# Mamba2 scan and PReLU MLP: chunk pairs 4 and 5 in two token blocks on half of the partitions, B and C of pair 4 turned by VectorE

## Chip, cores and metric

The kernel runs on one core of a Trainium2 chip. The metric is the device time of one execution in microseconds (us). TensorE is called PE here, its weight load PEld, VectorE DVE, ScalarE ACT, GpSimd POOL and the queue that issues most transfers SP. The granted TensorE clock was 1.000 over the whole profiled execution.

## The reference

Two blocks follow one another: a Mamba2 state-space scan in chunks, and an MLP with a PReLU whose slope is given for each hidden feature. Shapes: x is 4 x 8 x 768 x 32 (batch, heads H, tokens S, head width D), a is 4 x 8 x 768, B and C are 4 x 8 x 768 x 16 (state width N), w_in is 256 x 2048, w_out 2048 x 256, alpha 2048.

```python
log_a = np.log(np.clip(a, 1e-06, 1.0))
for c in range(nc):
    cum = np.cumsum(la, axis=-1)
    L = np.exp(cum[:, :, :, None] - cum[:, :, None, :]) * causal
    CB = np.einsum('bhin,bhjn->bhij', Cc, Bc)
    y_intra = np.einsum('bhij,bhjd->bhid', CB * L, xc)
    y_inter = np.einsum('bhin,bhnd->bhid', Cc, state) * np.exp(cum)[:, :, :, None]
    y[:, :, sl] = y_intra + y_inter
    Bx = np.einsum('bhjn,bhjd->bhjnd', Bc, xc) * np.exp(cum[:, :, -1:] - cum)[:, :, :, None, None]
    state = np.exp(np.sum(la, axis=-1))[:, :, None, None] * state + np.sum(Bx, axis=2)
...
h = y_as_tokens @ w_in            # 3072 x 2048
g = np.maximum(h, 0.0) + alpha * np.minimum(h, 0.0)
out = g @ w_out                   # 3072 x 256
```

## The kernel before

**Chunks, pairs, groups.** The kernel uses chunks of Q = 128 tokens, 24 of them: 6 for each of 4 batches. Two neighbouring chunks are a pair (0 to 11; pairs 0 to 2 are batch 0, 3 to 5 batch 1 and so on), and two pairs are a group of 512 tokens (0 to 5). The scan of a pair yields its 256 rows of the MLP's input, in the tile xT. Pairs 0 and 1 have a code of their own. All order is written out by hand: each engine executes its instructions in the order in which the program emits them, and waits at each for what it needs.

**What a pair needs.** For each head, the decays L are made by a scan on VectorE (L561 or L567, "dec<-abc"): the row of a, broadcast to all partitions by a transfer (abc, from the DRAM scratch z), is multiplied up from a one that stands on the diagonal of an identity matrix in PSUM (ident_p, one half of the bank m5_bank). B and C are needed with the state dimension on the partitions (bc). PE multiplies them for the gram products CB (L731 or L742); VectorE multiplies these by the decays (L753); and PE multiplies the result by x (L787 or L805) and adds the products of C with the old state (L779 or L797) into the same banks, the y products. ScalarE copies them into xT (L815 or L817). The state sums (L618 or L629) take bn, which is B times the decay to the chunk's end (GpSimd, L533, `pair_loads`); VectorE adds the old state (L642), GpSimd masks the sum (L645). GpSimd also makes cd, which is C times the decay from the chunk's start (L682).

**Two forms.** Pairs 2 to 5 use the whole form: a chunk's 128 tokens lie on 128 partitions. Pairs 6 to 11 (`gp >= HALF`, HALF = NP // 2 = 6) use the half form: chunk k lies on the partitions of half k, its tokens in two blocks of 64 (j = 0, 1). Decays and gram products of token block 1 with the queries of block 0 are zero and are left out, so that a head has 192 columns (SQ) for a chunk and not 256 for two: scans are 128x192 instead of 128x256, products 128x384 instead of 128x512. The matmuls use 64 or 32 rows by 32 or 64 columns of the PE array at places given by `tile_position`, several of them side by side. In the half form, the states and cd of a chunk are needed on the other half of the partitions as well; `moved` (L685) copies them there, cd by ScalarE and the masked state by GpSimd. The diagonal in ident_p is rearranged for the half form by `halve_identity` (two ScalarE copies), once, after pair 5's last scan. The rows of the scratch z of batches 2 and 3 are SQ = 192 wide: 128 values, and 64 more that begin the second block anew.

**B and C turned.** Pairs up to 4 transpose them on PE (four 128x128, L669) and copy the bank out by ScalarE (L672). Later pairs (`turned = gp > GC`, GC = 4) load them a second time in another layout and turn 32x32 blocks on VectorE (`turn_bc`, L574); `turn_bc(gp + 1)` is issued at the end of pair gp's products, with the first two scans of pair gp + 1 behind it.

**Two phases.** In the first, to about 78 us, the weights are loaded and converted, and for group 0 the MLP runs f by f (hidden L1095, output L1142), with pairs 1 to 3 between. What is issued after step f = 14 is `pair_loads(4)` and the rows of batches 2 and 3. Then follow `token_sums(1)` (L1183, "xs") and the first stages of pair 4. In the second phase the groups 1 to 5 run as 4 quads each (`quad`, z = 0 to 3), a Strassen-like product scheme with 7 products: matmuls L1241 into the PSUM tiles A and Y (both "hp", the pool ps_h with 2 buffers) and at times Z ("ss", the pool ps_s with 2 buffers), PReLU (`prelu`: L1224 on ScalarE, then L1226 on VectorE), differences on GpSimd (L1288, L1298) and matmuls L1216 into banks. The callback `after(j)` places the stages of the pairs of the next group among a quad's steps, by the table `steps`: pair 4 in quads z = 0 and 1 of group 1, pair 5 in z = 2 and 3. The gram products take two ss tiles and two hp tiles (`spare`), so they wait until PReLU has read A and Y. In group 1, GpSimd has in addition sums of weights (`weight_sums`, L1171, by the table `late_sums`), four in the first quad and four in the third (one of the first on VectorE).

**Loads.** `load_pair` issues a pair's transfers on SP: pair 4 at f = 10, pair 5 at the start of the first quad, pair 6 in the second, pair 7 in the fourth.

Of the kernel before, what the change touches and what calls it, by code (L numbers as in the profile page):

```python
# [9 lines left out]
F32 = mybir.dt.float32  # L10
# [12 lines left out]
def kernel(  # L23
# [25 lines left out]
    nc = tc.nc  # L49
# [4 lines left out]
    batch, H, S, D = x.shape  # L54
# [11 lines left out]
    GC = 4  # L66
# [10 lines left out]
    WQ = 256  # L77
    HQ = Q // 2
    SQ = Q + HQ
    HALF = NP // 2  # L80
    assert H * N == P and HD == d_model and KC == 2 and R == CPB == 6
    assert NCH % GC == 0 and GT == 512 and NF % 8 == 0 and d_model <= WQ

# [65 lines left out]
    def load_spread(gp, b, c):  # L149

        for w, t in enumerate(loads["p", gp][1] if gp >= HALF else ()):
            rows = scratch["z", b // 2].rearrange("(b h c) t -> b c h t", b=2, h=H)
            for k in range(2):
                nc.sync.dma_start(
                    out=t[HQ * k : HQ * (k + 1), : 4 * SQ].rearrange("p (h t) -> p h t", h=4),
                    in_=rows[b % 2, c + k, 4 * w : 4 * w + 4].unsqueeze(0)
                    .to_broadcast([HQ, 4, SQ]))
        for k, t in enumerate(loads["p", gp][1] if gp < HALF else ()):
            rows = scratch["z", b // 2].rearrange("(b h c) t -> b c h t", b=2, h=H)[b % 2, c + k]
            nc.sync.dma_start(out=t.rearrange("p (h t) -> p h t", h=H),  # L160
                              in_=rows.unsqueeze(0).to_broadcast([P, H, Q]))
            yield

    def load_products(gp, ap):
# [5 lines left out]
    def load_pair(gp, decays=True, parted=False):  # L170


        b, c = divmod(2 * gp, CPB)
        turned = gp > GC
        nat = ldx.tile([P, 3, 2, H * N], F32, name="nat")
        xt = ldx.tile([P, 2, HD], F32, name="xt")

        ap = ldx.tile([P, 2 * Q], F32, name="ap")
        if gp == 0:
            load_a(ap, b, c)  # L180
        elif gp > NB:
            load_products(gp, ap)
        if gp == 0:
            load_rows(0, nc.scalar)
        abc = []
        if gp >= HALF:
            load_tokens(nat[:, 0], B[b], c * Q)
        def load_bc(k):
            ts = slice((c + k) * Q, (c + k + 1) * Q)
            for i, src in enumerate((B,) if turned else (B, C)):  # L190
                eng = nc.scalar if gp == 0 and i else nc.sync
                eng.dma_start(out=nat[:, i, k].rearrange("p (h n) -> p h n", h=H),  # L192
                              in_=src[b, :, ts, :].rearrange("h p n -> p h n"))

        def load_x(k):
            ts = slice((c + k) * Q, (c + k + 1) * Q)
            nc.sync.dma_start(out=xt[:, k].rearrange("p (h d) -> p h d", h=H),  # L197
                              in_=x[b, :, ts, :].rearrange("h p d -> p h d"))

        for k in range((1 if parted else 2) if gp < HALF else 0):  # L200
            load_bc(k)
            if gp >= NB:
                load_x(k)
        for k in range(2 if gp < NB else 0):
            load_x(k)
        if gp == 0:
            nc.scalar.dma_start(out=al_n, in_=moe_alpha.rearrange("(k p) -> k p", p=P))
            loads["a", 1] = prep.tile([P, 2 * Q], F32, name="a1")
            load_a(loads["a", 1], b, c + 2)
        for i, src in enumerate((B, C) if turned else ()):  # L210


            for e in range(2):
                first = src[b, e : e + 1, c * Q : (c + 2) * Q, :]
                nc.sync.dma_start(out=nat[:, 1 + e, i],
                                  in_=bass.AP(tensor=first.tensor, offset=first.offset,
                                              ap=[[2 * S * N, P // 32], [8 * N, 32], [1, 8 * N]]))
        for k in range(2 if gp >= NB else 0):
            abc.append(lda.tile([P, H * Q], F32, name="abc"))
        loads["p", gp] = nat, abc, xt, ap  # L220
        if gp >= HALF:
            load_tokens(xt, x[b], c * Q)
        if decays:
            for part in load_spread(gp, b, c):
                pass
        return lambda: load_bc(1), lambda: load_x(1)
# [194 lines left out]
    def halve_identity():  # L421

        for s in range(2):
            nc.scalar.copy(
                out=ident_p[0][HQ:].rearrange("p (a s t) -> p s a t", a=2, s=2)[:, s],
                in_=ident[HQ:, HQ * (1 - s) : HQ * (2 - s)].unsqueeze(1).to_broadcast([HQ, 2, HQ]))
# [45 lines left out]
    def rows_out(i):  # L472


        if i == 0:
            scratch["z", 0] = dr.tile([RW, Q], F32, name="z0")
            nc.sync.dma_start(out=scratch["z", 0], in_=held.pop("z"))
            return
        d0 = held.pop(i)[:, :SQ]
        rpf = prep.tile([RW, Q], F32, name="rpf")  # L480
        nc.vector.tensor_tensor_scan(out=rpf, data0=d0[:, :Q], data1=zeros[:RW], initial=1.0,
                                     op0=ALU.mult, op1=ALU.add)
        nc.vector.memset(d0[:, :1], 0.0)
        for key, t in (("z", d0), ("pf", rpf)):
            scratch[key, i] = dr.tile([RW, t.shape[1]], F32, name=f"{key}{i}")
            nc.sync.dma_start(out=scratch[key, i], in_=t)

    def rows_short(r):

# [31 lines left out]
    def pair_loads(gp):  # L521

        b, c = divmod(2 * gp, CPB)
        nat, abc, xt, ap = loads["p", gp]

        bn = work.tile([P, 2, H * N], F32, name="bn")
        i, bi = divmod(b, 2)
        if gp >= HALF:
            pj = prt[i].rearrange("p (j b m h) -> p j b m h", j=2, b=2, h=H)[:, :, bi, c // 2]
        else:  # L530
            pj = (prt[i if gp >= NB else "short"]
                  .rearrange("p (b h c) -> p b c h", b=2, h=H)[:, bi, c : c + 2])
        nc.gpsimd.tensor_tensor(  # L533
            out=bn.rearrange("p k (h n) -> p k h n", h=H),
            in0=nat[:, 0].rearrange("p k (h n) -> p k h n", h=H),
            in1=pj.unsqueeze(3).to_broadcast([P, 2, H, N]), op=ALU.mult)
        return bn
# [43 lines left out]
    def pair(gp):  # L581
# [27 lines left out]
        def added_halves(banks):  # L609


            dps = [t[:, : 4 * D].rearrange("p (k m) -> p k m", k=2) for t in banks]
            for j in range(2):
                for r in range(4):
                    rs, hs = slice(32 * r, 32 * r + 32), slice(2 * r * D, 2 * (r + 1) * D)
                    for k in range(nk):
                        ks = slice(HQ * k, HQ * (k + 1))
                        nc.tensor.matmul(dps[k][rs, k], bn[ks, j, rs], xt[ks, j, hs],  # L618
                                         start=False, stop=j == 1,
                                         tile_position=(HQ * k, 32 * r),  # L620
                                         skip_group_check=True)
            return dps
# [131 lines left out]
            if i == 1:  # L754
                yield
        if fine and gp + 1 < NP:
            if gp + 1 == HALF:
                halve_identity()
                halved.append(True)
            turn_bc(gp + 1)  # L760
        yield

# [660 lines left out]
    def convert_next(first=True, **kw):  # L1423


        i = done[0]
        if i < len(pieces):
            convert(*pieces[i], **kw)
            if first and i and i + 2 < len(pieces):
                convert_a(*pieces[i + 2])  # L1430
            if loaded[0] == i + 6:
                load_next()
        done[0] += 1
# [20 lines left out]
    for f in range(FIRST, NF):  # L1454
        if f in (5, 10):
            load_pair(3 + f // 10)
        if f == 5:
            load_rows(1)
        hidden(0, f)
        for part in range(2):  # L1460
            if part:
                if f <= 10:
                    ssm(2)
                if f >= 9:
                    ssm(3)
            for i in CONVERTED.get((f, part), ()):
                if isinstance(i, str):
                    convert_a(*pieces[int(i)])
                else:
                    convert_next(first=False)  # L1470
        if f == 14:
            bns[4] = pair_loads(4)
            rows_clamp(1)
            held["pr"] = rows_scan(1)
            rows_out(1)
        if f == 8:
            bns[3] = pair_loads(3)
        output(f - FIRST)
        if f in in_steps:
            weight_sums(wi, in_sums, 0, in_steps[f])  # L1480
    early[0] = None
    beside[GC] = m5_bank[0][:, : 2 * Q]
    token_sums(1)
    ssm(2 * GC // 2, 4)

# [94 lines left out]
```

## Time and profile before

| What | Value |
|---|---|
| time, median of 3 runs | 355.99 us (355.93 to 356.35) |
| the profiled execution, first to last instruction | 355.9 us |
| PE busy | 349.3 us (98%) |
| PEld busy | 284.4 us (80%) |
| DVE busy | 235.8 us (66%) |
| POOL busy | 204.4 us (57%) |
| ACT busy | 171.8 us (48%) |
| one half-form scan (L561, 128x192) | 522 ns, mean of 48 |
| one whole-form scan (L567, 128x256) | 664 ns, mean of 32 |
| one turn on DVE (L574, 128x512) | 1114 ns, mean of 7 |
| one product of the half form (L753, 128x384) | 548 to 553 ns |
| one product of the whole form (L753, 128x512) | 681 to 685 ns |

Of the span's other executions the profile tells nothing; the profiled one differs by 0.1 us from the median of the runs. Groups of instructions are named by line, engine, operation and tile, out<-in. A matmul in f32 is recorded as two passes, so counts of matmuls in the chain are twice those in the code. A busy PE is not PE at its peak: ends of matmuls are modelled.

### The profile page before, as it was taken

Reading aid. Unit: us, or ns where it says so; the run is one execution under the profiler, and the core shown is the slowest. Engines: PE = TensorE matmul, PEld = TensorE weight load, DVE = VectorE, ACT = ScalarE, POOL = GpSimd, SP = SyncE. Lnnn points to the kernel's source line nnn. Section 1 sums busy time; section 2 is a strip of 40 time slices with the busy share of each in tenths; the row PEclk is TensorE's granted clock in tenths of the full one; section 3 lists DMA queues with packets and bytes.
Section 4 is the critical chain, followed back from the end, with each engine's and each line's share of the span. In section 5 each row is a group of like instructions: output and inputs, shape, how many; then the busy total and the mean of one; then the engine's idle time right before and its main releaser. Section 6 shows DMA issues by size and latency. Waiting matters only on the chain.

```text
span 355.9 us, 7778 instructions
## 1 busy us (share of the span) xinstructions
PE 349.3 (98%) x2985; PEld 284.4 (80%) x2985; DVE 235.8 (66%) x482; ACT 171.8 (48%) x391; POOL 204.4 (57%) x228
## 2 busy tenths in 40 slices
PE   8899999999999999999999999999999999999996
PEld 4576665578788888888888888888888888888885
DVE  6876986998748756847747856757856633643363
ACT  3477576535355346345345445345445344443431
POOL 6776568589939855725646626637526535434520
PEclk9999999999999999999999999999999999999999
DMA  7899989607345403503423423422001001001102
GB/s 138 182 202 270 329 174 279 148 17 159 106 83 128 102 3 75 104 2 77 78 57 74 86 51 71 85 55 65 11 2 31 0 2 29 2 1 31 31 0 59
DMA packets 105581, 30.24 MB, mean 85 GB/s; under 512 B 79896, under 2 KB 101448, under 8 KB 105544
## 3 DMA queue, kind: packets, MB, share of 16 engines
q1 hardware_dynamic: 103048, 29.43, 36.3%
q10 hardware_dynamic: 2496, 0.32, 0.6%
q8 instruction: 23, 0.38, 0.5%
q14 instruction: 14, 0.11, 0.1%
HBM read 26.32 MB, written 3.42 MB: 84 GB/s over the span
## 4 chain that ended last, share of the span: by engine, by line
PE 89%; SPq 4%; DMA 3%; DVE 2%; ACT 1%; POOL 1%; issue 0%; DVEq 0%; ACTq 0%
PE bank L1216 33%; PE hp L1241 29%; PE bank L1142 6%; PE ss L1241 6%; PE hp L1095 3%; DMA raw<-in_moe_w_in_dram 2%; SPq L192 2%; PE ss L787 1%; PE ss L731 1%; PE hp L1110 1%; PE bank L1209 1%; PE ss L805 1%; PE ss L779 1%; DMA xt<-in_x_dram 1%; SPq L197 1%; PE ss L742 1%
## 5 line engine op out<-in xcount | busy, mean ns | idle before, releaser
L1298 POOL TENSOR_TENSOR gt<-gt 128x512 f32<-128x512 f32 x58 | 74.2, 1279 | 21.1 <-DVE gt L1226 16.3
L1216 PE MATMUL bank<-gt,w_out 128*128 128x256 f32 x320 | 83.5, 381 | 0.0
L1216 PEld LDWEIGHTS bank<-gt,w_out 128*128 128x128 f32 x320 | 60.1, 190 | 9.2 <-issue 1.0
L1288 POOL TENSOR_TENSOR gt<-gt 128x512 f32<-128x512 f32 x20 | 25.4, 1269 | 62.5 <-DVE gt L1226 49.7
L1226 DVE SCALAR_TENSOR_TENSOR gt<-hp,s_mul,gt 128x256 f32<-128x256 f32 x96 | 42.0, 479 | 29.1 <-ACT gt L1224 26.8
L1224 ACT ACTIVATE gt<-hp,s_alpha 128x256 f32<-128x256 f32 x96 | 40.3, 471 | 34.5 <-PE hp L1241 31.4
L1216 PE MATMUL bank<-gt,ws 128*128 128x256 f32 x224 | 55.9, 379 | 0.0
L1216 PEld LDWEIGHTS bank<-gt,ws 128*128 128x128 f32 x224 | 42.3, 190 | 5.6
L1241 PE MATMUL hp<-xs,w_in 128*128 128x256 f32 x160 | 41.9, 384 | 0.0
L1241 PE MATMUL hp<-xs,ws 128*128 128x256 f32 x160 | 41.1, 380 | 0.0
L1267 DVE TENSOR_TENSOR hp<-hp,u 128x512 f32<-128x512 f32 x20 | 14.0, 700 | 35.2 <-ACT u L1265 35.2
L1241 PEld LDWEIGHTS hp<-xs,ws 128*128 128x128 f32 x160 | 30.3, 190 | 4.3 <-POOL xs L1183 0.2
L1241 PEld LDWEIGHTS hp<-xs,w_in 128*128 128x128 f32 x160 | 29.7, 190 | 4.5
L1142 PE MATMUL bank<-w_out,gt 128*128 128x256 f32 x128 | 31.1, 385 | 0.4 <-POOL w_out L330 0.4
L1142 PEld LDWEIGHTS bank<-w_out,gt 128*128 128x128 f32 x128 | 23.6, 190 | 7.2 <-issue 2.9
L1241 PE MATMUL ss<-xT,w_in 128*128 128x256 f32 x96 | 24.6, 379 | 0.0
L645 POOL TENSOR_TENSOR sm<-state,bmask 128x256 f32<-128x256 f32 (+1 forms) x10 | 6.2, 620 | 29.0 <-DVE state L642 29.0
L1095 PE MATMUL hp<-xT,w_in 128*128 128x512 f32 x48 | 22.8, 596 | 0.0
L561 DVE TENSOR_TENSOR_SCAN dec<-abc,bank 128x192 f32<-128x192 f32 x48 | 22.7, 522 | 0.0
L1256 ACT COPY m<-hp 128x512 f32<-128x512 f32 x8 | 4.7, 586 | 35.7 <-PE hp L1241 35.7
L1265 ACT COPY u<-hp 128x512 f32<-128x512 f32 x20 | 11.7, 585 | 19.4 <-PE hp L1241 19.4
L1226 DVE SCALAR_TENSOR_TENSOR gt<-c,s_mul,gt 128x256 f32<-128x256 f32 x40 | 20.6, 555 | 0.0
(232 smaller groups left out, 608.2 us busy)
## 6 DMA issues: line engine op xcount, KB each, us to landing
abc<-z SPq DMA_DIRECT2D x24, 192.0 KB
raw<-in_moe_w_in_dram SPq DMA_DIRECT2D x8, 512.0 KB
raw<-in_moe_w_out_dram SPq DMA_DIRECT2D x8, 512.0 KB
abc<-z SPq DMA_DIRECT2D x8, 512.0 KB
out_dram<-o_sb SPq DMA_DIRECT2D x32, 64.0 KB
nat<-in_B_dram SPq DMA_DIRECT2D x26, 64.0 KB
xt<-in_x_dram SPq DMA_DIRECT2D x12, 128.0 KB
xt<-in_x_dram SPq DMA_DIRECT2D x24, 64.0 KB
```

The source lines that it names most:

```text
L192: eng.dma_start(out=nat[:, i, k].rearrange("p (h n) -> p h n", h=H), in_=src[b, :, ts, :].rearrange("h p n -> p h n"))
L561: nc.vector.tensor_tensor_scan(out=dv[:, o : o + SQ], data0=abc[k][:, s : s + SQ], data1=ident_p[0][:, :SQ], initial=0.0, op0=ALU.mult, op ...
L1095: nc.tensor.matmul(hp, w_in[:, k, f * P : (f + 1) * P], xts[g][:, k], start=(k == 0), stop=(k == KC - 1))
L1142: nc.tensor.matmul(pos[0][t // 2][:, t % 2], gt[:, t * Q : (t + 1) * Q], w_out[:, f], start=(f == 0 and t % 2 == 0), stop=(f == NF - 1), s ...
L1216: nc.tensor.matmul(ms[g][i][:, h], w, blocks[g, z][n][:, p], start=(q == 0 and h == 0), stop=(q == NQ - 1), skip_group_check=True)
L1224: nc.scalar.mul(o[:, p], h[:, p], s_alpha[:, fs[p]])
L1226: nc.vector.scalar_tensor_tensor(out=o[:, p], in0=h[:, p], scalar=s_mul[:, fs[p]], in1=o[:, p], op0=ALU.mult, op1=ALU.max)
L1241: nc.tensor.matmul(to[:, p], w(2 * z + p), b, start=start and p == 0, stop=True, skip_group_check=True)
L1265: nc.scalar.copy(out=u2, in_=A)
L1267: nc.vector.tensor_tensor(out=Y, in0=Y, in1=u2, op=ALU.add)
L1288: nc.gpsimd.tensor_tensor(out=tc_, in0=g22, in1=g12, op=ALU.subtract)
L1298: eng.tensor_tensor(out=o, in0=x0, in1=x1, op=ALU.subtract)
```

## The change

HALF becomes GC = 4, so that pairs 4 and 5 use the half form, and pair 4 is turned by VectorE too. What this needs for batches 0 and 1 (rows of the scratch that are 192 wide, `rows_halved`; the decays to the chunk's end in the half layout, `turned_halved`, a tile "prh") is added; `halve_identity` and the turn of pair 4 move ahead of the second phase; pair 4's state sums go to two banks instead of one. `z0` keeps 128 of its 192 columns from `rows_out(0)`, and the other 64 are stored at f = 8 on SP, behind a GpSimd copy of 96x63.

```diff
-    HALF = NP // 2
+    HALF = GC
...
-                              in_=rows.unsqueeze(0).to_broadcast([P, H, Q]))
+                              in_=rows[:, :Q].unsqueeze(0).to_broadcast([P, H, Q]))
...
-        turned = gp > GC
+        turned = gp >= HALF
...
-            scratch["z", 0] = dr.tile([RW, Q], F32, name="z0")
-            nc.sync.dma_start(out=scratch["z", 0], in_=held.pop("z"))
+            scratch["z", 0] = dr.tile([RW, SQ], F32, name="z0")
+            nc.sync.dma_start(out=scratch["z", 0][:, :Q], in_=held.pop("z"))
...
+    def rows_halved():
+        d0 = held.pop(0)
+        nc.gpsimd.tensor_copy(out=d0[:, Q + 1 :], in_=d0[:, HQ + 1 : Q])
+        nc.sync.dma_start(out=scratch["z", 0][:, Q:], in_=d0[:, Q:])
+
+    def turned_halved():
+        t = prep.tile([P, RW // 2], F32, name="prh")
+        for v in range(2):
+            for j in range(2):
+                js, vs = (slice(HQ * i, HQ * (i + 1)) for i in (j, v))
+                nc.scalar.copy(
+                    out=t[vs].rearrange("p (j h m) -> p j h m", j=2, h=H)[:, j],
+                    in_=prt[0][js].rearrange("p (b h m k) -> p b k h m", b=2, h=H, k=2)[:, 1, v])
+        prt["half"] = t
...
-        if gp >= HALF:
+        if HALF <= gp < NP // 2:
+            pj = prt["half"].rearrange("p (j h m) -> p j h m", j=2, h=H)[:, :, :, c // 2]
+        elif gp >= HALF:
...
-                                         start=False, stop=j == 1,
+                                         start=gp == HALF and j == 0, stop=j == 1,
...
-            if gp + 1 == HALF:
-                halve_identity()
-                halved.append(True)
             turn_bc(gp + 1)
...
+        if f == 8:
+            rows_halved()
         if f == 14:
+            turned_halved()
             bns[4] = pair_loads(4)
...
     early[0] = None
-    beside[GC] = m5_bank[0][:, : 2 * Q]
+    beside[GC] = m5_bank[0][:, : 2 * Q], ss_tile()
+    halve_identity()
+    halved.append(True)
+    turn_bc(GC)
     token_sums(1)
     ssm(2 * GC // 2, 4)
```

On the engines' queues this gives, for each of the pairs 4 and 5: 17 transfers on SP (before: 9 for pair 4, 11 for pair 5); on VectorE scans of 192 and products of 384 columns; on ScalarE two more copies (cd) between cz and the PReLU activations that follow; on GpSimd two more copies (the masked state) behind cd.

## Prediction, made before the changed kernel ran

> **What bounds the kernel now.** I read the page first: engine totals, and the chain of work that ended last.
>
> ```profile
> PE 349.3 (98%) x2985; PEld 284.4 (80%) x2985; DVE 235.8 (66%) x482; ACT 171.8 (48%) x391; POOL 204.4 (57%) x228
> PE 89%; SPq 4%; DMA 3%; DVE 2%; ACT 1%; POOL 1%; issue 0%; DVEq 0%; ACTq 0%
> ```
>
> PE is busy 349.3 of 355.9 us and is 89% of the chain; what is not PE lies almost wholly before 46 us and after 350. So from there on a microsecond of PE work removed is a microsecond won, if nothing makes PE wait in its place. Hence two questions: how much PE work goes, and who is then late. For the first I read the chain in order of time, 76 to 132 us (pairs 4 and 5 as they are) and 132 to 190 us (pairs 6 and 7, already in the half form). Columns: start, us, what; x counts hardware passes, two per instruction.
>
> ```profile
> 77.70 0.36 PE bank L629 x16
> 78.06 0.58 PE ss L669 x4
> 78.64 0.87 PE ss L1241 x4
> 79.51 0.95 PE hp L1241 x4
> ...
> 97.44 0.60 PE ss L797 x32
> 98.03 1.01 PE ss L805 x32
> 99.05 0.11 PE ss L629 x8
> 99.16 1.92 PE hp L1241 x8
> ```
>
> ```profile
> 179.53 0.60 PE ss L779 x32
> 180.13 0.79 PE ss L787 x48
> ...
> 181.19 1.92 PE hp L1241 x8
> ```
>
> The whole form of the y products takes 0.60 + 1.01, the half form 0.60 + 0.79. For the second question I read the order of time of each other engine around the places that the change touches. Columns: start, us, engine, line, operation, and in brackets the idle time before it and what ended it. GpSimd before the first quad:
>
> ```profile
> 76.48 0.75 POOL L533 TENSOR_TENSOR bn<-nat,prt 128x256 f32<-128x256 f32 x1
> 77.20 1.38 POOL L1171 TENSOR_TENSOR w_in<-w_in 128x512 f32<-128x512 f32 x1
> 78.55 0.73 POOL L1183 TENSOR_TENSOR xs<-xT 128x256 f32<-128x256 f32 x1
> ```
>
> The first xs ends at 79.28, and PE's first matmul that uses one starts at 79.51: one weight load (190 ns) later. PE is already held by GpSimd here. VectorE some 20 us earlier:
>
> ```profile
> 56.84 0.69 DVE L308 SCALAR_TENSOR_TENSOR wr<-wt,wr 128x512 uint32<-128x512 uint32 x1 [3.08 <-POOL wt L278]
> ...
> 64.72 0.74 DVE L1099 SCALAR_TENSOR_TENSOR gt<-hp,s_mul,gt 128x512 f32<-128x512 f32 x1
> ```
>
> It waits for GpSimd at 56.84 and then runs without a gap to 65.46, where L1099 frees the bank of PE's next L1095 (65.64; 1.86 us in the chain where its neighbours take 1.72, so PE waits some 0.14 there). Last the quad in which pair 5 is scanned (the third, 105 to 119 us), GpSimd, then VectorE:
>
> ```profile
> 113.82 0.73 POOL L682 TENSOR_TENSOR cd<-bc,ap 128x256 f32<-128x256 f32 x1
> 114.51 1.27 POOL L1171 TENSOR_TENSOR ws<-w_out,ws 128x512 f32<-128x512 f32 x1
> 115.75 1.45 POOL L1171 TENSOR_TENSOR w_out<-w_out 128x512 f32<-128x512 f32 x1
> ```
>
> ```profile
> 115.41 2.07 DVE L1226 SCALAR_TENSOR_TENSOR gt<-c,s_mul,gt 128x256 f32<-128x256 f32 x2
> 117.40 0.86 DVE L1226 SCALAR_TENSOR_TENSOR gt<-hp,s_mul,gt 128x256 f32<-128x256 f32 x2
> ```
>
> The second VectorE row ends at 118.26 and frees the hp bank A, which pair 5's gram products take at 118.49: 0.2 us of room.
>
> **Part by part.** Before-clock throughout; later times move with PE.
>
> (1) *The added GpSimd copy of 96x63* stands between the wt at 51.57 and bn at 52.33, where GpSimd runs back to back to 56.80. What queues behind it is bn (wanted only at 55.2), a weight sum, w_in (wanted at 60.9) and the wt that VectorE waits for at 56.84. So the delay goes to VectorE, through its gapless run to L1099, and to PE at 65.64; later the conversions chain back to GpSimd's xs, so PE's 0.5 us of slack there does not absorb it. The size is not in the trace: the nearest rows are copies of 64x128 (287 ns, start to start 0.35) above and memsets of one column (0.10) below. I take **+0.25** (0.10 to 0.35), near the copy.
>
> (2) *Pair 4 turned by VectorE.* Four PE transposes go (0.58), and the state sums take 0.39 (pair 6's L618) instead of 0.36. PE then reaches the xs-using matmul 0.55 earlier and waits for GpSimd's 79.28, which nothing in the change moves forward: **0** (at best -0.09, its 0.95 against the usual 0.86). VectorE gets a transpose of 1.11 and eight scans of 0.52 for eight of 0.66; up to the L1267 at 82.92 that is 0.95 + 0.9 + 0.5 + 1.9 from 78.25, so 82.5, and L1267 waits for ScalarE's u till 82.88 anyway. Without that cover each 0.1 us would eat the 1 us until PE needs it at 84.61. ScalarE loses a copy of 0.58, gains the two identity copies (0.56) before it, and four small copies (0.24 each) after 72.83, in an idle stretch of 3.18: bn of pair 4, which now reads them, starts at 76.48, long after.
>
> (3) *Gram products, pair 4.* 89.96 to 91.19 is 1.23; pairs 6 to 11 take 0.84 (146.18 to 147.02). But A is free only at 90.02 (VectorE's L1226 at 89.14 takes 0.88), so the end is about 90.05 + 0.85: **-0.29** (-0.39 to -0.10). Here cd ends at 85.39 and the new ScalarE copies delay the next activations by 0.36; the idle 0.96 before 88.27 takes that.
>
> (4) *y products of pair 4 and state sums of pair 5.* 97.44 to 99.16 is 1.72; the same two steps for pairs 7 and 8 are 179.53 to 181.19, 1.66: **-0.06**. The state sums get dearer (0.11 to about 0.26).
>
> (5) *Gram products, pair 5.* PE work 1.08 (118.54 to 119.62) becomes 0.84: -0.24. Against it stands a new wait. ScalarE gets two copies of cd (0.60 together) after cz, ahead of the six activations of the quad's end. cd ends at 114.55, since two weight sums lie before it on GpSimd, while ScalarE is free at 112.67 and started the next activation at 113.69. Behind the copies: activations from 115.20 instead of 113.69 (0.72 + 0.95 + 0.84), the last ends at 117.7; VectorE's L1226 pairs follow at 116.1 and 116.9. GpSimd's two copies (0.63) push its w_out sum to 116.4 to 117.87. The row of 2.07 (0.87 in undisturbed quads) lost 1.2 in 1.79 us beside GpSimd's sums, so it moves at a third; 0.95 us of overlap leaves its end at 118.4, the next pair's at 119.2. PE wants A at 118.5: a wait of **0.7**, between 0.1 (no slowing: 117.8 + 0.8) and 1.1 (VectorE stands until 117.87: 118.74 + 0.85). Term **+0.46** (-0.14 to +0.86). GpSimd's own followers (gt at 117.62, bn, three gt) move 0.9, and it then idles 4.87.
> [...]
>
> (6) *y products of pair 5, state sums of pair 6.* 125.00 to 126.99 is 1.99; pairs 8 and 9 have 206.60 to 208.35, 1.75: **-0.24**.
>
> (7) *Loads.* SP issues 17 transfers for pair 4 (9 before) after one small store of z, 17 for pair 5 (11), packets fewer. Pair 4's were issued by 64.15; eight more at 0.6 to 0.7 (rows at 96 to 110) end near 70, and are wanted at 78.2. Pair 5's begin at 78.56 and, at pair 6's pace (13 us with its waits), end at 91.6; the first decays land about 92, VectorE scans them at 94.2, and has 1.64 idle before 97.28. Behind them SP has the store of the output tile ready at 89.58, which nobody waits for soon. **0**.
>
> Sum: 0.25 + 0 - 0.29 - 0.06 + 0.46 - 0.24 = **+0.12**. The profiled execution's span is 355.9, 0.1 below the median 355.99; the difference is added to the median: 356.1. All low ends: 0.10 - 0.09 - 0.39 - 0.06 - 0.14 - 0.24 = -0.82; all high ends: 0.35 + 0 - 0.10 - 0.06 + 0.86 - 0.24 = +0.81.
>
> **Rivals.** 0.2% (0.7 us) is about what a measurement of this kernel can tell from no change.
> *The PE savings come through* (17%): terms 3 to 6 without waits are -0.39 - 0.06 - 0.24 - 0.24 = -0.93, and a copy of 0.10 leaves -0.83: 355.2. For it: pairs 6 to 11 run the same form with no PE wait. Against: there cd ends before ScalarE's cz does (139.79 against 140.57), since no weight sums lie in GpSimd's way.
> *The ScalarE block at pair 5 decides* (25%): if A comes free after 119.8, the wait exceeds 1.3 and outweighs the rest, +0.7 with the other terms at my values. At 1.4, with a GpSimd copy of 0.35: 0.35 - 0.29 - 0.06 - 0.24 + 1.4 - 0.24 = +0.92, 356.9. For it: in the third quad ScalarE, VectorE and GpSimd follow one another with 0.2 us of room. Against: even a VectorE at a standstill ends at 119.6.
> *Late loads of pair 5* are in those 25%: they cost only beyond 96.3 us (97.28 less a scan pair of 0.94), 4 us later than I have them.
>
> **Numbers.** Forecast, no change that can be told: 58%, 356.1. Faster by over 0.2%: 17%; slower: 25%. Range 355.2 to 356.9, the two rivals' times; it takes in the ends of the sums.
>
> **What would show it.** Right: PE's work on pairs 4 and 5 falls by about 1.5 us, yet PE shows idle time of about 0.5 before the first xs matmul and about 0.7 inside pair 5's gram products, where the releaser is VectorE's L1226; ScalarE waits for cd in the third quad; VectorE's first wait for wt after 50 us ends 0.25 later. Wrong: no PE gap at pair 5 (then faster), the first quad's xs no later than before, or a VectorE transpose waiting for a transfer.

## Result, and the profile after

The changed kernel is slower: 361.21 us, median of 6 runs (358.89 to 361.86), against 356.37 us for the kernel before (6 runs, 355.93 to 358.22). The ratio is 1.012, 95% interval 1.0099 to 1.0141. The prediction had 356.1 us and a range up to 356.9.

The profiled execution of the changed kernel spans 360.1 us. From L487 on, lines stand 16 to 22 lower in the file: L1241 is now L1257, L1142 is L1158, L1095 is L1111, L1226 is L1242, L618 is L637, L1171 is L1187. The gram products of pairs 4 and 5, L742 before, are now those of the half form, L750 (L731 before). In the experiments an edit can move them by one more.

The engine totals of the page, the summary of its chain, and the row of the clock that TensorE was granted in 40 slices of 9 us:

```profile
PE 350.8 (97%) x3101; PEld 286.0 (79%) x3101; DVE 236.1 (66%) x483; ACT 173.5 (48%) x398; POOL 205.7 (57%) x233
PE 83%; DVE 5%; DMA 3%; POOL 3%; SPq 2%; issue 1%; ACT 1%; DVEq 0%; POOLq 0%; ACTq 0%
PEclk9999999998999999999999999999999999999999
```

PE was to lose some 1.5 us of work; its busy time grew by 1.5 (349.3 to 350.8), and the chain has 5% of VectorE where it had 2%. In one slice, the tenth (81 to 90 us), the clock row shows an 8. The chain in order of time, around that slice (start, us, what):

```profile
65.17 2.00 PE hp L1111 x4
...
80.06 0.27 PE bank L637 x2
...
80.79 1.52 PE ss L1257 x4
82.31 1.71 PE hp L1257 x4
84.02 1.25 PE bank L1158 x4
```

Two things stand here. Between the two upper rows the chain leaves PE, and comes back to it at 80.06 with pair 4's state sums (L637). And the three rows after them take 1.52, 1.71 and 1.25, where before they took 0.87, 0.95 and 0.86.

To compare the executions piece by piece, I count all times from one mark: the first y product of pair 2 (49.55 before, 49.08 after), since what lies ahead of it differs from trace to trace: the mark stands at 47.72 to 49.55 in the twelve traces of this document, and at 49.55 and 48.96 in two kernels that are the same up to there. It also sets right a comparison made ahead of the result: in the runs that list both, the time is 1.7 to 1.8 us longer than the span (361.86 against 360.1). A span of 355.9 therefore belongs to a time of about 357.6, and the profiled execution before was not 0.1 us off its median. The steps of the prediction then become stretches of the chain:

| Stretch (step of the prediction) | Before | After | Change | Predicted |
|---|---|---|---|---|
| mark to the end of the hidden row at 65.64 / 65.17 (1) | 17.95 | 18.09 | +0.14 | +0.25 |
| from there to pair 4's gram products (2) | 22.46 | 26.73 | **+4.27** | 0 |
| gram products, pair 4 (3) | 1.23 | 0.98 | -0.25 | -0.29 |
| y products 4, state sums 5 (4) | 1.72 | 1.66 | -0.06 | -0.06 |
| from their end to the end of gram products, pair 5 (5) | 20.46 | 21.08 | +0.62 | +0.46 |
| y products 5, state sums 6 (6) | 1.99 | 1.75 | -0.24 | -0.24 |
| mark to the end of these | 77.44 | 81.90 | +4.46 | +0.12 |

The whole loss lies in one stretch. What holds PE there is read from the other engines. VectorE, then PE's weight loads and PE, then GpSimd, each in order of time (start, us, engine, line, operation; in brackets the idle time before and what ended it):

```profile
77.92 1.10 DVE L593 STREAM_TRANSPOSE bc<-nat 128x512 f32<-128x512 f32 x1
78.86 0.94 DVE L580 TENSOR_TENSOR_SCAN dec<-abc,bank 128x192 f32<-128x192 f32 x2
```

```profile
80.03 0.14 PEld L637 LDWEIGHTS bank<-xt,bn 64*32 64x32 f32 x2 [3.07 <-POOL xs L1199]
80.06 0.27 PE L637 MATMUL bank<-xt,bn 64*32 64x64 f32 x2 [2.70 <-DVE dec L580]
```

```profile
76.18 0.75 POOL L552 TENSOR_TENSOR bn<-nat,prh 128x256 f32<-128x256 f32 x1
76.90 1.38 POOL L1187 TENSOR_TENSOR w_in<-w_in 128x512 f32<-128x512 f32 x1
78.23 0.72 POOL L1199 TENSOR_TENSOR xs<-xT 128x256 f32<-128x256 f32 x1
```

PE's last matmul before ended at 77.36, and its next instruction, L637, starts at 80.06: 2.70 us idle. The weight load names GpSimd's xs as its releaser, which L637 doesn't read; bn, which it does read, was ready at 76.93. What ends just ahead of 80.03 is VectorE's pair of scans (78.86 + 0.94 = 79.80), and PE's own row names them: 2.70 idle, ended by dec of L580. They read the diagonal ident_p, one half of m5_bank; L637 writes the other half of that bank. The program makes L637 wait for VectorE, and what stands behind L637 on PE starts after it: the first quad's row stands at 80.79 in the chain above. Since all of m5_bank is one tile, no run here tells whether the program orders by the bank or by the tile.

The granted clock after the idle time, in stretches of the same trace (stretch, its length, busy time and instructions of PE, PEld, DVE, ACT, POOL, then the clock):

```profile
77.00:80.06 3.06, 0.36 (x3) 0.03 (x1) 2.76 (x6) 0.00 (x0) 2.98 (x4) 1.00 0.22 63
80.06:82.30 2.24, 2.23 (x37) 1.77 (x38) 1.32 (x4) 0.00 (x0) 1.74 (x3) 0.77 0.54 76
82.30:84.00 1.70, 1.70 (x6) 1.34 (x5) 1.04 (x3) 0.57 (x1) 1.62 (x3) 0.50 0.34 51
84.00:85.30 1.30, 1.30 (x6) 1.07 (x5) 0.00 (x0) 0.59 (x1) 1.30 (x2) 0.74 0.26 77
85.30:87.00 1.70, 1.70 (x9) 1.50 (x8) 0.14 (x1) 0.59 (x1) 1.50 (x4) 1.00 0.63 128
```

The clock falls after the idle stretch and is whole again by 85.3. The 0.77 is a mean: in the trace's record of the clock it is 1.00 up to 81.25, 1.2 us after PE went on, and 0.50 from there to 84.67. So the +4.27 has two parts: up to the start of the first quad's first row +2.48 (13.62 after the hidden row, 11.14 before), and +1.80 in the three slow rows (4.48 against 2.68).

Pair 5's gram products, by PE's weight loads, ScalarE and VectorE of the changed kernel:

```profile
122.99 0.14 PEld L750 LDWEIGHTS hp<-cz,bc 32*64 32x64 f32 x2 [0.67 <-DVE gt L1242]
```

```profile
118.22 0.60 ACT L709 COPY shifted<-cd 64x128 f32<-64x128 f32 x2 [1.92 <-POOL cd L701]
```

```profile
119.76 0.88 DVE L1242 SCALAR_TENSOR_TENSOR gt<-hp,s_mul,gt 128x256 f32<-128x256 f32 x2 [1.89 <-POOL shifted L711]
120.56 1.59 DVE L1242 SCALAR_TENSOR_TENSOR gt<-c,s_mul,gt 128x256 f32<-128x256 f32 x2
```

These are the waits of step 5: ScalarE 1.92 for cd, VectorE behind it, the activation from c and gt slowed to 1.59, and PE's weight loads 0.67 inside the gram products.

### The profile page after: what moved, and what is told of

Read it like the earlier page. It is cut to its first block, busy times and chain, and to the rows that moved or that the text cites. A ratio compares the mean times of both kernels' runs of the same rounds, so it can differ in the third digit from the quotient of the medians.

```text
span 360.1 us, 8041 instructions
## 1 busy us (share of the span) xinstructions
PE 350.8 (97%) x3101; PEld 286.0 (79%) x3101; DVE 236.1 (66%) x483; ACT 173.5 (48%) x398; POOL 205.7 (57%) x233
## 4 chain that ended last, share of the span: by engine, by line
PE 83%; DVE 5%; DMA 3%; POOL 3%; SPq 2%; issue 1%; ACT 1%; DVEq 0%; POOLq 0%; ACTq 0%
PE bank L1232 31%; PE hp L1257 27%; PE ss L1257 5%; PE bank L1158 5%; PE hp L1111 2%; DMA raw<-in_moe_w_in_dram 2%; PE ss L803 2%; SPq L192 1%; PE ss L750 1%; PE ss L795 1%; PE hp L338 1%; PE hp L1126 1%; POOL gt L1314 1%; DVE gt L1242 1%; PE bank L1225 1%
## 5 line engine op out<-in xcount | busy, mean ns | idle before, releaser
L1242 DVE SCALAR_TENSOR_TENSOR gt<-hp,s_mul,gt 128x256 f32<-128x256 f32 x96 | 42.0, 478 | 31.0 <-ACT gt L1240 27.2
L1257 PE MATMUL hp<-xs,ws 128*128 128x256 f32 x160 | 41.9, 385 | 0.0
L1257 PE MATMUL hp<-xs,w_in 128*128 128x256 f32 x160 | 41.9, 384 | 0.0
L1257 PEld LDWEIGHTS hp<-xs,ws 128*128 128x128 f32 x160 | 31.0, 194 | 4.4
L1257 PEld LDWEIGHTS hp<-xs,w_in 128*128 128x128 f32 x160 | 29.7, 190 | 4.5
L1158 PE MATMUL bank<-w_out,gt 128*128 128x256 f32 x128 | 31.6, 388 | 0.4 <-POOL w_out L330 0.4
L580 DVE TENSOR_TENSOR_SCAN dec<-abc,bank 128x192 f32<-128x192 f32 x64 | 30.3, 524 | 0.0
L1158 PEld LDWEIGHTS bank<-w_out,gt 128*128 128x128 f32 x128 | 24.0, 193 | 7.3 <-issue 2.9
L1257 PE MATMUL ss<-xT,w_in 128*128 128x256 f32 x96 | 25.2, 386 | 0.0
L1111 PE MATMUL hp<-xT,w_in 128*128 128x512 f32 x48 | 22.7, 596 | 0.0
L1291 DVE TENSOR_TENSOR c<-hp,m 128x512 f32<-128x512 f32 x20 | 13.8, 692 | 10.6 <-PE hp L1257 10.6
```

Of the source, the lines that this page charges most:

```text
L580: nc.vector.tensor_tensor_scan(out=dv[:, o : o + SQ], data0=abc[k][:, s : s + SQ], data1=ident_p[0][:, :SQ], initial=0.0, op0=ALU.mult, op ...
L1111: nc.tensor.matmul(hp, w_in[:, k, f * P : (f + 1) * P], xts[g][:, k], start=(k == 0), stop=(k == KC - 1))
L1158: nc.tensor.matmul(pos[0][t // 2][:, t % 2], gt[:, t * Q : (t + 1) * Q], w_out[:, f], start=(f == 0 and t % 2 == 0), stop=(f == NF - 1), s ...
L1242: nc.vector.scalar_tensor_tensor(out=o[:, p], in0=h[:, p], scalar=s_mul[:, fs[p]], in1=o[:, p], op0=ALU.mult, op1=ALU.max)
L1257: nc.tensor.matmul(to[:, p], w(2 * z + p), b, start=start and p == 0, stop=True, skip_group_check=True)
L1291: nc.vector.tensor_tensor(out=c22, in0=A, in1=m5, op=ALU.add)
```

## Experiments

All ratios are to the kernel before, run beside the experiment; the intervals are of 95%.

**Another bank for the sums.** The first of pair 4's two banks of state sums is one that holds no diagonal.

```diff
-    beside[GC] = m5_bank[0][:, : 2 * Q], ss_tile()
+    beside[GC] = bank(2)[:, : 2 * Q], ss_tile()
```

> The changed kernel, with the first of pair 4's two state-sum tiles put into another PSUM bank (bank 2) and not beside the identity in m5_bank. Theory (L637 waits for VectorE's first two scans only because they read the identity from the same bank): PE's idle stretch before L637 shrinks from 2.7 us to almost none, about 0.5 us of idle appears in its place before the first xs matmul, the granted clock stays at 1.00 throughout (0.91 in 80 to 100 us with the change), VectorE's scans still start near 78.9; the span falls by 3 to 4 us, from 360.1 to about 356.5, ratio to the kernel before 0.998 to 1.004, with about 0.7 of wait left inside pair 5's gram products. Rival A (PE waits for a late transfer of pair 4, or for GpSimd's bn or xs): the idle stretch stays at 2.5 to 3 us and the ratio near 1.012. Rival B (the clock drops whatever PE waits for, for the half form as such): the wait goes, the clock still drops, ratio about 1.005.

357.36 us (356.38 to 358.31, 10 runs), ratio 1.0025 (1.0007 to 1.0042). The stretch (2) is 22.47, as before the change (22.46). The wait for the scans is gone, and with it the low clock (1.00 from 60 to 85). PE's weight loads now wait first for bn and then for xs:

```profile
75.91 0.10 PEld L637 LDWEIGHTS bank<-xt,bn 64*32 64x32 f32 x1 [0.33 <-POOL bn L552]
77.63 0.73 PEld L1257 LDWEIGHTS hp<-xs,ws 128*128 128x128 f32 x4 [0.61 <-POOL xs L1199]
```

That is the picture that the prediction drew: weight loads that stand 0.61 us for xs, where it had 0.55. From the mark to the end of step 6 it is 77.72, +0.28 on before, near the +0.12 of the sum.

**The same bank, the sums first.** Here the bank stays, and the sums are issued ahead of what else uses it.

```diff
-        scan_half(decs[gp], loads["p", gp][1], 0, 0)
+        if scan:
+            scan_half(decs[gp], loads["p", gp][1], 0, 0)
...
+    halved.append(True)
+    turn_bc(GC, scan=False)
+    dec4 = decs[GC]
+    ssm(GC)
     halve_identity()
-    halved.append(True)
-    turn_bc(GC)
+    scan_half(dec4, loads["p", GC][1], 0, 0)
     token_sums(1)
-    ssm(2 * GC // 2, 4)
+    ssm(GC, 3)
```

> The changed kernel, with m5_bank kept for the state sums, but pair 4's state sums issued on PE before the identity is halved and before the first two scans; only VectorE's transpose stays ahead of them. Theory (same bank, so the order of scans and matmul decides): L637 no longer waits for VectorE, the idle stretch before it falls below 0.5 us, the clock stays at 1.00, ScalarE's two identity copies now wait for L637 (near 78) and VectorE's scans start at 79.0 or little later; ratio 0.998 to 1.004, within 0.5 us of the variant with another bank. Rival A (a late transfer or GpSimd): no change from 1.012.

357.35 us (356.55 to 357.88, 10 runs), ratio 1.0022 (1.0008 to 1.0036); stretch (2) is 22.47 once more. Two different cures of the shared bank give the same time. A late bn or late transfers would have left both as slow as the change.

**PE kept busy while it waits.** Six matmuls on constants, whose result nobody uses, stand ahead of L637; the wait for the scans stays.

```diff
-    beside[GC] = m5_bank[0][:, : 2 * Q], ss_tile()
+    own4 = ss_tile()
+    beside[GC] = m5_bank[0][:, : 2 * Q], own4
+    keep_warm(own4[:, 2 * Q :], 6)
```

> The changed kernel, with six added matmuls on constants (128x256, about 0.43 us each, 2.6 together) issued on PE before pair 4's state sums, into the unused half of their second bank, so that PE is busy while it waits. Theory (the lower clock after the wait is a result of PE's idling, and costs about 1.9 us by the stretched rows 1.52, 1.71 and 1.25 against 0.86 each): the wait for the scans remains, L637 still starts near 80.0, but the clock stays at 1.00 and the rows behind it take 0.86 to 0.95; span about 358.2, ratio 1.005 to 1.008. Rival (the clock drops for another reason, or the rows are slow for another reason): span near 360.1, ratio 1.011 to 1.013. If the constants run past the scans' end the time grows by that.

359.32 us (359.14 to 360.35, 4 runs), ratio 1.0078 (1.005 to 1.0105). The chain:

```profile
76.83 2.61 PE ss L338 x12
...
79.97 1.06 PE ss L1257 x4
81.03 0.86 PE hp L1257 x4
81.90 0.86 PE bank L1158 x4
```

L637 starts as late as with the change (12.89 us behind the hidden row in both traces), but the quad's rows take 1.06, 0.86 and 0.86, not 1.52, 1.71 and 1.25, and the clock stays at 1.00 (77 to 85 us). So 1.70 us (4.48 less 2.78) belong to the low clock, as a consequence of PE's idling; 3.41 us at half clock come to the same. Stretch (2) is 24.76, +2.30 on before for the wait. What is left of the +4.27, 0.28 us, lies in the state sums: 0.73 with the change and 0.45 here, at a clock of 1.00 in both. Why they took longer isn't shown. The medians agree (359.32 against 361.21). One of the six runs of the changed kernel itself had a mean clock of 1.000 where the others had 0.995, and it is the one of 358.89 us.

**cd earlier.** With the other bank, and GpSimd's cd issued at the pair's first scans, so that it isn't behind two weight sums.

```diff
+                    if k == 0 and w == 0:
+                        c_decayed()
                     if k == 1 and w == 1:
                         spread_c()
-                        c_decayed()
```

> The variant with another bank, and besides cd of pairs 4 to 11 computed by GpSimd in the first scan stage of a pair, so that in the third quad it stands before the two weight sums. Theory (at pair 5 ScalarE stands still behind cd, so A comes free 0.7 us late): ScalarE's wait of 1.92 us before the copies of cd goes, L1242 of the quad's end is done before PE wants A, PE's 0.67 wait inside L750 goes; 0.6 to 0.8 us less than the variant with another bank, ratio to the kernel before 0.996 to 1.001. Rival (the weight sums beside VectorE's two-SBUF-input L1242 hold it up anyway): the wait stays at 0.4 to 0.7 and nothing is won. For the other pairs, whose cd does not stand behind weight sums, no change.

357.05 us (356.0 to 358.36, 10 runs), ratio 1.0013 (0.9993 to 1.0033). Step 5 falls only from +0.60 to +0.37. ScalarE no longer waits for cd, but VectorE and GpSimd, in order of time:

```profile
112.57 0.88 DVE L1243 SCALAR_TENSOR_TENSOR gt<-hp,s_mul,gt 128x256 f32<-128x256 f32 x2 [0.32 <-POOL ws L1188]
113.36 2.92 DVE L1243 SCALAR_TENSOR_TENSOR gt<-c,s_mul,gt 128x256 f32<-128x256 f32 x2
116.21 0.86 DVE L1243 SCALAR_TENSOR_TENSOR gt<-hp,s_mul,gt 128x256 f32<-128x256 f32 x2
```

```profile
113.33 1.27 POOL L1188 TENSOR_TENSOR ws<-w_out,ws 128x512 f32<-128x512 f32 x1
114.56 1.45 POOL L1188 TENSOR_TENSOR w_out<-w_out 128x512 f32<-128x512 f32 x1
```

VectorE's activation from c and gt starts earlier, falls almost wholly beside two weight sums, and takes 2.92 where its neighbours, which read PSUM, take 0.88 and 0.86. Taken one by one, its two instructions end at 114.88 and 116.28, each 0.28 us behind the end of a sum (114.60 and 116.00): by these ends each of them lasts until the sum beside it is done. Bank A comes free hardly earlier, as the rival of the expectation had it.

**The row copy on ScalarE.** In addition, the 96x63 copy leaves GpSimd.

```diff
-        nc.gpsimd.tensor_copy(out=d0[:, Q + 1 :], in_=d0[:, HQ + 1 : Q])
+        nc.scalar.copy(out=d0[:, Q + 1 :], in_=d0[:, HQ + 1 : Q])
```

> The kernel of the run before with cd early (state sums in another bank, cd early), and the 96x63 row copy on ScalarE in place of GpSimd. If the copy's place on GpSimd is what delays VectorE and so PE (term 1, +0.12 to +0.14 by the rows of the runs so far), then the chain's hp row of the third hidden chunk after the gram products of pair 3, 1.97 to 2.00 with the copy on GpSimd, goes back to 1.86, and the stretch from the first y products of pair 2 to the end of that row is 17.95 (before) and not 18.07; the ratio falls by 0.04%, too little to be seen in the times. Rival: the 1.97 has another cause (bn or ScalarE): the row stays.

356.92 us (356.15 to 357.95, 12 runs), ratio 1.0004 (0.9988 to 1.002). The row went from 1.97 to 1.91, not to 1.86, and stretch (1) to 18.00 (17.95 before, 18.06 with cd early alone). Single traces scatter, but the groups don't overlap: the six kernels with the copy on GpSimd have 18.05 to 18.09, the four with it on ScalarE 17.97 to 18.01, and the two without it 17.95 and 17.97. The direction is that of term 1, and on GpSimd the copy costs some 0.1 us.

**Two weight sums later.** The kernel with the other bank and cd early, and the third quad's last two weight sums behind that quad's gt sums.

```diff
-                 (2, 6): ((wqt, out_sums, 4, 2),), (2, 8): ((wqt, out_sums, 4, 3),)}
+                 (2, 11): ((wqt, out_sums, 4, 2),), (2, 12): ((wqt, out_sums, 4, 3),)}
```

> The kernel with the state sums in another bank and cd early, and the last two weight sums of the third quad (w_out's third and fourth, 1.27 and 1.45) issued behind the quad's four gt sums, where GpSimd idles 4.1 us. If it is GpSimd's weight sums beside VectorE's activation from c and gt that hold bank A: that activation pair goes from 2.92 to about 0.9, PE's wait for gt inside pair 5's gram products goes (0.4 to 0), the gram products take 0.85 to 0.95 instead of 1.44, ratio some 0.15% below the run with cd early alone, about 1.000. If the wait comes from ScalarE's queue or from VectorE's own order instead: the activation pair is short, but the gram products still take over 1.2.

356.01 us (355.4 to 357.73, 12 runs), ratio 0.9994 (0.9977 to 1.0011). VectorE:

```profile
114.96 0.87 DVE L1243 SCALAR_TENSOR_TENSOR gt<-c,s_mul,gt 128x256 f32<-128x256 f32 x2
```

The same instruction pair takes 0.87 instead of 2.92; pair 5's gram products take 0.84, no weight load waits for gt, and step 5 is -0.24: the saving of PE work alone.

**xs first.** The kernel with the other bank, cd early and the row copy on ScalarE, and the weight sum on w_in issued behind the xs.

```diff
-        if f in in_steps:
+        if f in in_steps and f != 14:
             weight_sums(wi, in_sums, 0, in_steps[f])
...
     token_sums(1)
+    weight_sums(wi, in_sums, 0, in_steps[14])
```

> The kernel with the state sums in another bank, cd early and the row copy on ScalarE, and GpSimd's weight sum on w_in ahead of the first quad (1.38) issued behind the four xs. If PE's saved transposes of pair 4 are lost to the wait for xs, as the prediction has it: the wait before the first xs matmul goes (the row of 77.65 ended 0.73 later than one 0.86 after the ss row before it), and the ratio falls by up to 0.2% against the run with the row copy on ScalarE alone. Rival: PE then waits for w_in's sum, now 1.4 later, at the fifth product of the quad, or for another engine just behind: the time is the same and another row of the quad is longer than 0.87.

357.14 us (356.17 to 357.84, 12 runs), ratio 1.0007 (0.9989 to 1.0025): no gain in the time. In the trace the wait for xs is gone and stretch (2) is 22.00, -0.46. But pair 4's gram products take 1.38 instead of 0.98, so that 0.40 is given back at once: the rival, with its wait somewhat further on than it was thought to be.

**All four edits** (xs first and the two sums later, with the bank, cd and the copy).

> All of these together: state sums in another bank, cd early, row copy on ScalarE, xs first, weight sums later. With no wait left, the terms are -0.25 (gram of pair 4), -0.07, -0.24 (gram of pair 5), -0.25 and up to -0.7 at xs: about -1.5 us or 0.4% under the kernel before, ratio 0.996. If waits only move on, 0.999 to 1.001.

356.43 us (355.56 to 357.03, 12 runs), ratio 0.9987 (0.9972 to 1.0002): between the two expectations. The gram products of pair 4 still take 1.37. VectorE's activation from c and gt in the first quad takes 2.28 there, beside two weight sums of GpSimd.

**The first quad's sums too.** All of these, and two weight sums of the first quad behind its gt sums.

```diff
-                 (0, 6): ((wqt, out_sums, 0, 2),), (0, 8): ((wi, in_sums, 4, 0),),
+                 (0, 11): ((wqt, out_sums, 0, 2),), (0, 12): ((wi, in_sums, 4, 0),),
```

> The kernel with all four edits, and the last two weight sums of the first quad (w_out's third, 1.27, and the first of w_in's second half, 1.45) also issued behind that quad's gt sums. With xs first, pair 4's gram products took 1.37 where they take 0.98 otherwise, and VectorE's activation pair from c and gt took 2.28 beside these two sums. If it is the same mechanism as in the third quad: that pair takes about 0.9, the gram products 0.84 to 0.9, and the stretch from the first y products of pair 2 to the start of the third half's products after pair 5 (76.59 with the four edits, 77.44 before the change) falls to about 76.1; ratio to the kernel before 0.997 to 0.998. Rival: the sums, now later, delay bn of pair 5 or the second quad, and the time is given back there.

355.28 us (354.92 to 357.25, 12 runs), ratio 0.9968 (0.9948 to 0.9988): faster than the kernel before. VectorE:

```profile
85.25 0.87 DVE L1243 SCALAR_TENSOR_TENSOR gt<-c,s_mul,gt 128x256 f32<-128x256 f32 x2
```

By stretches: +0.06, -0.45, -0.25, -0.06, -0.24, -0.24. From the mark to the end of step 6 it is 76.25 where it was 77.44: -1.19, and the medians differ by 0.88 (356.16 to 355.28). The mechanism is the one of the third quad: the pair takes 0.87, not 2.28. The gram products took 0.98, not the 0.84 to 0.90 that were expected, so the 76.1 was missed by 0.15. Nothing is given back behind: up to VectorE's last instruction the trace is 301.80 from the mark, 302.99 before.

**The moves without the change.** The kernel before, with xs first and the four weight sums moved, but pairs 4 and 5 in the whole form.

> The kernel before the change, with the moves of GpSimd's weight sums alone (w_in's behind the xs, two of the first and two of the third quad behind the gt sums), to see whether the gain of the four edits belongs to the change or to the moves. By the trace of before, PE waits 0.08 for xs and 0.06 for bank A at pair 4, and not at pair 5: the moves can win 0.1 to 0.2 us, which the times can't show (ratio 0.999 to 1.000), so that what the other kernel wins beyond that belongs to the half form of pairs 4 and 5. Rival: the moves help as much here, ratio 0.997 to 0.998, and the change itself brings nothing.

356.28 us (355.57 to 358.37, 12 runs), ratio 0.9996 (0.9975 to 1.0016); 77.38 from the mark, -0.06. The moves bring nothing by themselves. The half form of pairs 4 and 5 is worth some 1.1 us of PE time (77.38 less 76.25; the medians differ by 1.00), and needs the moves to show it. cd early and the row copy were not tried on the kernel before; its trace shows no wait of PE at pair 5 that an earlier cd could take away.

## Why the prediction was wrong, step by step

**Step 2 failed, and it alone made the sign.** The prediction put it as "PE then reaches the xs-using matmul 0.55 earlier and waits for GpSimd's 79.28, which nothing in the change moves forward: 0". It followed VectorE's new transpose and scans forward, to what VectorE itself does later (the L1267 at 82.92), and asked of PE only whether its work falls and whether xs is there. It didn't ask what PE's next instruction, the first state sum, now waits for. With `halve_identity` and `turn_bc(GC)` issued ahead of it, that instruction stands behind two scans that read another half of the bank it writes. The profile of before had the pieces: VectorE free at 78.25, a turn of 1.11, two scans: about 80.1, against PE's 77.70. Worked out, that wait alone was some 2.4 us, well past the high end. Both bank experiments show the cause. The low clock that followed, 1.70 us, was no term either; the trace of before has no PE gap over 0.85 us behind the program's first matmul from which it could have been read, but a wait of over 2 us, longer than any there, should have carried an open end above. No rival named this wait.

**Step 2's other half was right.** With the bank out of the way the change's saved transposes are lost to xs: weight loads wait 0.61, and the stretch is 22.47 against 22.46. Moving xs forward brings the 0.46 back.

**Step 1** was too dear: +0.14 for +0.25. The copy took 0.76 on GpSimd, above its high end of 0.35, but bn behind it took 0.63 where it had 1.14. VectorE's wait for wt ended 0.13 later from the mark (7.42 against 7.29), half of what its test asked. The copy causes most of it: in the traces with the copy on ScalarE the stretch is 0.04 to 0.12 shorter than in those with it on GpSimd.

**Steps 3, 4 and 6** hold to 0.04.

**Step 5** had the mechanism and nearly the size, +0.62 for +0.46: ScalarE waited 1.92 for cd and PE's weight loads 0.67 for bank A; by the stretch, with 0.24 of work saved, PE's wait was 0.86 where 0.7 was predicted. Its reading that VectorE moves at a third beside GpSimd's sums was wrong, and that it came so near is in part luck: only one sum lay beside the activation. In the trace of before the two activations of the row of 2.07 end at 116.07 and 117.48, 0.29 and 0.28 behind the ends of the sums at 115.78 and 117.20. By these ends they lasted until the sums were done, as its upper end of 1.1 assumed. What it had in a smaller part decides more: with cd early the same wait came back from the weight sums beside the activation from c and gt, and moving those sums took it away.

**Step 7:** no VectorE transpose or scan of pairs 4 and 5 waits for a transfer. Without the bank, the forecast "no change that can be told" would have been nearly right in the stretches (+0.28) and somewhat low in the time (1.0025).

## What to carry to other kernels

When work moves ahead of an engine's next instruction, take that instruction first and list what each bank, tile and queue it touches now stands behind; here m5_bank, one tile in PSUM, counted as one: the first state sum, which writes one half of it, waited 2.70 us for scans that read the other half, and did not wait for them in another bank. A wait on an otherwise busy PE cost more than its length here: the 2.70 us idle were followed by rows that took 1.70 us more. Saved work on the bounding engine was had here only when the next late engine was moved too (76.25 us from the mark with the moves, 77.72 with the other bank alone), and the moves did next to nothing without the change that they serve (77.38 against 77.44).

## What the hardware showed that was not expected

An idle time of 2.70 us was followed by 3.41 us of half clock, in which PE's rows took 1.52, 1.71 and 1.25 us instead of 0.87, 0.95 and 0.86. Five of six runs have the mean clock that this gives (3.41 x 0.5 / 360.1 is 0.005). In the traces' record of the clock, of the changed kernel and of the kernel before, it is 1.00 for 75.09 us (to 81.25), 0.50 for 3.41 and 1.00 for 276.48 in the former, and 1.00 for 351.57 in the latter: 22, 1, 81 and 103 times 3.413 us. In the 3.41 us before the clock fell (77.84 to 81.25), PE was 2.23 without a matmul. How long an idle time must be to lower the clock isn't shown, nor that one of 2.70 us always does: one run is at 1.000, and only one run of the changed kernel was traced.

VectorE's activation from c and gt doesn't go on slowly beside GpSimd's sums: in the traces of the kernel before and of the changed kernel, each of the 14 that take over 0.6 us (0.47 to 0.48 alone) ends 0.28 or 0.29 us behind the end of a sum that ran beside it. The 96 activations from hp in each of these two traces take 0.49 at most, beside such sums too. So a pair of those from c and gt that takes 0.87 alone took 2.92 with cd early.
